# Scaling v on VectorE in place of Pool, with a refitted order model and new ranks, in a fused DeltaNet and low-rank mixer kernel

## The chip, the cores and the metric

The kernel runs on one core of one Trainium2 chip. The metric is the device time of one execution in microseconds. The time before is the median of three runs.

## The reference

Two layers follow each other. The first is a delta-rule attention over 4 batches, 8 heads, 768 steps and a head dimension of 48, the second a mixer over the result, laid out as 4 x 768 x 384:

```
k_n = k / (norm(k) + 1e-6)
for t in range(S):
    y[t]  = q[t] @ state
    v_old = k_n[t] @ state
    state = state + beta[t] * outer(k_n[t], v[t] - v_old)
x = y as (B, S, H*D)
...
h = x^T @ U @ V                       # rank 32, along the sequence
u = x + h^T
out = u + relu(u @ w_ch1) @ w_ch2     # 384 -> 1536 -> 384
```

## The kernel before, in words

The first layer is not run step by step. Chunks of 64 steps are solved at once, and a state is carried from chunk to chunk. The work is cut into 8 units: unit n is one half (six chunks) of batch n // 2, with all its heads. Two large buffers, slot_87 and slot_88 in the profile (both called slot there), hold the even and the odd units.

For a unit, SyncE's queue (SP) loads k, q, v and a second copy of k called z (L367, eight transfers of 72 KB for each of k, q and v, four for z). TensorE (PE) transposes k and q (L463) and makes products of them (L490); k's products give a triangular system. `norms` (L421) takes the norms of k out of the diagonal, makes their reciprocals on VectorE (DVE) and turns the norms into rows (L443); L446 multiplies v in place by those rows, and key "scaled" is then given. In place of dividing k by its norm, the kernel thus scales v. `blocks` (L549) inverts the triangular system: a substitution of pairs of small DVE operations (L581 and L587, 15 pairs in units 0 to 2 and 31 in the others), a transposition (L594), and for units 0 to 2 two further products on PE (L637, L651) whose result DVE takes back (L655, L603). Then PE joins the blocks (L677, L680, L695, L698), ACT copies (L685, L704, L716) and Pool clears corners (L723). `recur` (L732) first prepares each half of a unit (L796 and L807, which need the join, Pool's L723 and the scaled v), and then carries the state: for each chunk PE makes L845 (what the state gives for k), DVE subtracts it from v (z, L858), PE makes L873 from z and DVE adds it to the state (L883; L885 for the first); L760 and L774 make the outputs.

The weights of the second layer arrive as 64-bit floats. `load_weights` (L916) brings 14 slices and DVE rebuilds 32-bit floats in five operations a slice (L974, L980, L986, L992, L1002), with one of ACT (L959). Then, for each of four batches in three blocks of 256 rows, `front` makes the low-rank part (L1025, L1031, L1039, L1043, L1047, L1050), and `wide` the two large products: 36 matmuls of L1117 (72 records, each 32-bit product is recorded twice) and 42 of L1154, the second in a form with seven half-size products that need sums made by DVE (L1089, L1096); L1102 adds the result into X, and L1106 stores it. The PE work of the attention of batches 1 to 3 is placed between the matmuls of the mixer of the batch before.

What is decided ahead of the chip is the order of the instructions on each engine. Each piece of work is a generator that yields an estimated cost before it issues (`op`, L100), or names of results that it needs (`need`). `run` (L198) is a list scheduler with a model of the five engines: it keeps a clock for each, takes the pieces that can start soonest, and among those that start within a small hold (L227) the one with the lowest rank. Ranks come from the call (`place_of`, or a number), or from a table of overrides, PLACES (L140). The model knows [...] PE's change between tile shapes (SWITCH), instruction fetches (LOT, FETCH, `late`), and PE's half clock: `pace` (L176) counts the work in spans of 3.413 us that begin at one assumed phase, PHASE, and multiplies the cost of PE work by 1.9 after a span with little of it. The model never waits on the chip; it only fixes the order, and each engine then runs its queue in that order and waits on semaphores.

Of the kernel before, what the change touches and what calls it, by code (L numbers as in the profile page):

```python
# [26 lines left out]
def kernel(  # L27
# [20 lines left out]
    nc = tc.nc  # L48
# [33 lines left out]


    clock = dict(port=0.0, pe=0.8, dve=0.8, act=0.8, pool=0.8, sp=0.8)
    state = dict(now=0.0, mode=None, hw=0.0, slow=1.9, lot=69, fetched=0.0, flow=0.0, span=0)
    free = dict(pair={x: 0.0 for x in range(4)}, mix={})
    done, parts, waits, ready, last = {}, {}, {}, {}, {}
    asked, missing, awaited, woken = {}, {}, {}, []
    LAT = dict(pe=0.22, dve=0.06, act=0.06, pool=0.1, sp=0.0)
    SWITCH, HOLD = 0.18, 0.18  # L90
    LOT, FETCH = 256, 3.9
    SPAN, PHASE = 3.413, 1.44

    def dve(n):
        return (n + 151) / 960.0
# [17 lines left out]
    def emitted(key, after=0.0):  # L113
        done[key] = state["now"] + after
        for i in awaited.pop(key, ()):
            missing[i].discard(key)
            if not missing[i]:
                woken.append(i)
# [19 lines left out]
            waits[i] = s  # L138

    PLACES = """  # L140
    add_up b0 i0 60.5; add_up b1 i0 12.835; block b0 i1 c2 87.0; block b0 i1 c3 87.0
    block b1 i2 c4 90.229; blocks n1 17.5; diagonals n0 h0 18.353; diagonals n0 h1 18.353
    diagonals n2 h1 89.754; diagonals n3 h1 32.197; gather b0 i1 h1 c1 91.5; gather b1 i0 h0 c1 28.323
    gather b1 i1 h1 c0 28.323; grams n3 i0 -1.0; grams n3 i1 -1.0; grams n4 i0 9.835
    grams n6 i1 30.555; grams n7 i0 8.088; grams n7 i1 17.0; joins n3 h0 43.767
    load n1 namev halves(0, 1) 90.5; load n2 namev halves(0, 1) 90.5; norms n4 95.0; norms n6 17.663
    outputs b0 c0 74.0; outputs b0 c1 86.5; outputs b0 c10 85.5; outputs b1 c2 73.081
    outputs b1 c9 30.481; outputs b3 c0 -9.5; prepare n1 h0 -5.5; prepare n3 h1 58
    prepare n5 h0 -6.5; prepare n5 h1 -6.5; prepare n7 h0 55.06; prepare n7 h1 55.06
    products n1 i1 j1 70.0; products n2 i0 j0 87.293; products n2 i1 j0 39.279; products n2 i1 j1 60.538  # L150
    products n3 i1 j1 12.0; products n4 i1 j0 54.436; recur b1 49.374; recur b2 18.0
    seed n5 10.405; start i2 99.0; wide b0 i0 30.055; wide b2 i1 2.667
    """
    PLACES = dict(x.strip().rsplit(" ", 1) for x in PLACES.replace("\n", ";").split(";") if x.strip())

# [15 lines left out]
        return free[tag], [y for y in free[tag] if x is None or x == y]  # L171

    def cost_of(s):
        return s["cost"] * (state["slow"] if s["mode"] else 1.0)

    def pace(at, end, flow):  # L176

        while int((end - PHASE) / SPAN) > state["span"]:
            state["span"] += 1
            edge = PHASE + SPAN * state["span"]  # L180
            part = flow * min(1.0, max(0.0, (edge - at) / max(end - at, 1e-9)))
            used, flow, at = state["flow"] + part, flow - part, max(at, edge)
            if used > 0.36 * SPAN or "mixing" in done:
                state["slow"] = 1.0
            elif used < 0.28 * SPAN and "mixing" not in done:
                state["slow"] = 1.9
            state["flow"] = 0.0
        state["flow"] += flow

    def late(s, at):  # L190

# [6 lines left out]
    def run():  # L198
        stall = {}
        while waits or woken:  # L200
            while woken:
                i = woken.pop(0)
                at = max([0.0] + [done[x] for x in asked[i]])
                if at > ready[i]:
                    last[i] = None
                advance(i, None, max(at, ready[i]))
            some = {}
            for i, s in waits.items():
                e, was = s["e"], last.get(i)
                at = max(was[1] if was and was[0] == e else ready[i], clock[e])  # L210
                if s["port"]:
                    at = max(at, clock["port"])
                if s["take"]:
                    banks, of = places(s)
                    if not of:
                        continue
                    at = max(at, min(banks[y] for y in of))
                if s["mode"] and s["mode"] != state["mode"]:
                    at += SWITCH
                stall[i] = late(s, at)[1]  # L220
                some.setdefault(e, []).append((at + stall[i], i))
            picks = []
            for e, them in some.items():
                soon = min(at for at, _ in them)
                them.sort(key=lambda x: (not waits[x[1]]["rush"], x[1]))
                for at, i in them:
                    hold = 0.18 if i[0] < 13 else HOLD if i[0] < 90 else SWITCH  # L227
                    if at > soon + hold:
                        continue
                    if not any(a < at and a + waits[x]["cost"] < at + 0.05 for a, x in them):  # L230
                        picks.append((at, i))
                        break
            at, i = min(picks)
            at -= stall[i]
            s, got = waits[i], None
            if s["take"]:
                banks, of = places(s)
                got = min(of, key=lambda y: (banks[y], y))
                del banks[got]
            cost = cost_of(s)  # L240
            if s["e"] == "pe":
                crossed, more = late(s, at)
                state["lot"] += s["words"]
                if state["lot"] > LOT:
                    state["lot"] -= LOT
                    cost += more
                    behind = state["hw"] - crossed - more - 2.4
                    state["fetched"] = crossed + more + FETCH + max(0.0, behind)
                pace(at, at + cost, s["flow"])
            state["now"] = clock[s["e"]] = at + cost  # L250
            if s["port"]:
                clock["port"] = at + cost
            if s["mode"]:
                state["mode"] = s["mode"]
            for tag, x in s["give"]:
                free[tag][x] = state["now"] + s["lat"]
            last[i] = s["e"], state["now"]
            advance(i, got, state["now"] + s["lat"])
# [162 lines left out]
    def norms(n):  # L421

        _, _, _, _, _, vn, _, _ = units[n]
        b, hf = divmod(n, NU)
        flat = gs.rearrange("p s t -> p (s t)")
        yield need(("laid", n), ("seeded", n))
        yield op("act", 0.2)
        norm = small.tile([128, BK], FP32, name="norm")
        nc.scalar.sqrt(norm, flat[:, 0 : BK * BK : BK + 1])
        yield need(("betas", hf))  # L430
        yield op("dve", 1.15, port=True)
        nc.vector.tensor_scalar_add(norm, norm, 1e-6)
        rec = small.tile([128, BK], FP32, name="rec", bufs=1)
        nc.vector.reciprocal(rec, norm)
        nc.vector.tensor_tensor(out=rec, in0=rec, in1=rec, op=ALU.mult)
        nc.vector.tensor_tensor(out=cp[:, n % 2], in0=rec, in1=betas[:, hf, b], op=ALU.mult)
        nc.vector.tensor_copy(
            out=xt.rearrange("p s t -> p (s t)")[:, 0 : BK * BK : BK + 1], in_=cp[:, n % 2]
        )
        emitted(("c", n))  # L440
        yield op("dve", 0.2)
        rows = small.tile([128, BK], FP32, name="norm_rows")
        nc.vector.transpose(rows, norm)  # L443
        yield landed("v", n)
        yield op("pool", 2.2)
        nc.gpsimd.tensor_tensor(  # L446
            out=vn.rearrange("p c (r j) d -> p r c j d", r=2),
            in0=vn.rearrange("p c (r j) d -> p r c j d", r=2),
            in1=rows[:, 0:CS].rearrange("p (r c j) -> p r c j", r=2, c=UC)[
                :, :, :, :, None  # L450
            ].to_broadcast([128, 2, UC, 2, D]),
            op=ALU.mult,
        )
        emitted(("scaled", n), 0.2)

    def grams(n, i):
        kn, kq, pg, qk, qn, _, diag, _ = units[n]
# [91 lines left out]
    def blocks(n):  # L549
# [26 lines left out]
        nc.vector.tensor_tensor(out=gb, in0=gb, in1=by, op=ALU.mult)  # L576
        for j in range(size - 1):
            m, w = j + 1, size - 1 - j
            yield op("dve", 2 * dve(split * m * w), port=True)
            prod = single.tile([128, split, m, w], FP32, name="prod", tag="prod")  # L580
            nc.vector.tensor_tensor(  # L581
                out=prod,
                in0=gb[:, :, j : j + 1, j + 1 :].to_broadcast([128, split, m, w]),
                in1=xb[:, :, 0:m, j : j + 1].to_broadcast([128, split, m, w]),
                op=ALU.mult,
            )
            nc.vector.tensor_tensor(  # L587
                out=xb[:, :, 0:m, j + 1 :], in0=xb[:, :, 0:m, j + 1 :], in1=prod,
                op=ALU.subtract,
            )  # L590
# [625 lines left out]
```

## Time and profile before

| | us |
|---|---|
| median of 3 runs | 626.62 (626.53 to 628.6) |
| the profiled execution | 629.01 |
| its span, first to last instruction | 627.2 |
| PE busy | 589.1 (94%) |
| DVE busy | 393.7 (63%) |
| ACT busy | 227.4 (36%) |
| POOL busy | 47.3 (8%) |
| first matmul of the mixer's first product (L1117) | starts at 114.93 |
| mean granted clock of TensorE | 0.940 |

The profile tells one execution. Busy times are sums over an engine's instructions; a share is of the span, and says nothing on which stage an engine bounds. A line such as L446 is a line of the kernel; out<-in are tile names, 128x1152 is partitions by elements, and a number in brackets at a line's end is how long the engine was idle ahead of it and what ended that. 64*64 ahead of a matmul's shape is the part of the array that it uses. The changed file is 13 lines longer from the order model on, so that its L459 stands for L446 of this one.

### The profile page before, as it was taken

Reading aid. Unit: us, or ns where it says so; the run is one execution under the profiler, and the core shown is the slowest. Engines: PE = TensorE matmul, PEld = TensorE weight load, DVE = VectorE, ACT = ScalarE, POOL = GpSimd, SP = SyncE. Lnnn points to the kernel's source line nnn. Section 1 sums busy time; section 2 is a strip of 40 time slices with the busy share of each in tenths; the row PEclk is TensorE's granted clock in tenths of the full one; section 3 lists DMA queues with packets and bytes.
Section 4 is the critical chain, followed back from the end, with each engine's and each line's share of the span. In section 5 each row is a group of like instructions: output and inputs, shape, how many; then the busy total and the mean of one; then the engine's idle time right before and its main releaser. Section 6 shows DMA issues by size and latency. Waiting matters only on the chain.

```text
span 627.2 us, 23410 instructions
## 1 busy us (share of the span) xinstructions
PE 589.1 (94%) x10536; PEld 519.3 (83%) x10536; DVE 393.7 (63%) x957; ACT 227.4 (36%) x450; POOL 47.3 (8%) x69
## 2 busy tenths in 40 slices
PE   5598879899989999999999999999999999999997
PEld 5498867688779888888887878898989869898987
DVE  4979877988989528998995883459923123131312
ACT  3745556522252553255147227331130431101020
POOL 3031010001200100013002001010000000000000
PEclk9855557999989999999999999999999999999999
DMA  8570666750000050450043034000000000000000
GB/s 125 104 160 4 204 172 145 183 125 28 3 4 5 28 97 3 93 102 8 15 82 68 3 74 80 12 24 6 1 26 14 17 2 2 25 1 27 13 13 26
DMA packets 101572, 33.26 MB, mean 53 GB/s; under 512 B 90528, under 2 KB 101280, under 8 KB 101472
## 3 DMA queue, kind: packets, MB, share of 16 engines
q1 hardware_dynamic: 99712, 31.18, 22.1%
q8 instruction: 82, 1.34, 0.8%
q10 hardware_dynamic: 1600, 0.30, 0.3%
q0 software_dynamic: 160, 0.30, 0.2%
q14 instruction: 18, 0.15, 0.1%
HBM read 27.03 MB, written 4.72 MB: 51 GB/s over the span
## 4 chain that ended last, share of the span: by engine, by line
PE 72%; DVE 20%; issue 3%; ACT 2%; DMA 1%; SPq 1%; DVEq 0%; ACTq 0%
PE P L1154 24%; PE P L1117 23%; DVE xt L587 5%; DVE prod L581 5%; PE P L490 3%; PE P L796 2%; PE P L463 2%; PE P L845 2%; PE P L1039 2%; PE P L807 2%; PE P L873 2%; PE P L637 2%; DVE zz L594 2%; PE P L651 2%; PE P L760 1%
## 5 line engine op out<-in xcount | busy, mean ns | idle before, releaser
L1117 PE MATMUL P<-ut,w_sb 128*128 128x256 f32 x864 | 202.1, 387 | 0.6 <-ACT ut L1050 0.6
L1117 PEld LDWEIGHTS P<-ut,w_sb 128*128 128x128 f32 x864 | 161.4, 192 | 24.4 <-issue 1.2
L1154 PE MATMUL P<-w_sb,hs 128*128 128x192 f32 x720 | 125.9, 329 | 0.4 <-DVE X L1102 0.4
L1154 PEld LDWEIGHTS P<-w_sb,hs 128*128 128x128 f32 x720 | 117.2, 190 | 3.5 <-DVE X L1102 0.7
L1073 ACT ACTIVATE hs<-P 128x512 f32<-128x512 f32 x72 | 43.0, 597 | 149.7 <-PE P L1117 138.2
L587 DVE TENSOR_TENSOR xt<-xt,prod 128x112 f32<-128x112 f32 (+21 forms) x200 | 64.6, 323 | 6.9
L581 DVE TENSOR_TENSOR prod<-gs,xt 128x112 f32<-128x112 f32 (+21 forms) x200 | 64.4, 322 | 4.8
L1102 DVE TENSOR_TENSOR X<-X,P 128x192 f32<-128x192 f32 x84 | 29.5, 351 | 60.0 <-PE P L1154 59.3
L1089 DVE TENSOR_TENSOR S<-hs 128x384 f32<-128x384 f32 x24 | 16.7, 694 | 63.3 <-ACT hs L1073 63.3
L744 ACT COPY X<-P 64x192 f32<-64x192 f32 x96 | 30.0, 313 | 71.6 <-PE P L774 67.3
L1154 PE MATMUL P<-w_sb,S 128*128 128x192 f32 x288 | 51.1, 330 | 0.0
L1154 PEld LDWEIGHTS P<-w_sb,S 128*128 128x128 f32 x288 | 46.7, 190 | 1.1
L463 PE MATMUL P<-ident,slot 128*128 128x128 f32 x192 | 29.4, 304 | 10.9 <-POOL xt L566 5.1
L858 DVE TENSOR_TENSOR z<-slot,P 128x192 f32<-128x192 f32 x44 | 15.5, 353 | 37.7 <-PE P L845 27.8
L716 ACT COPY slot<-zz 32x384 f32<-32x384 f32 x64 | 32.6, 509 | 10.9 <-DVE zz L594 6.9
L463 PEld LDWEIGHTS P<-ident,slot 128*128 128x128 f32 x192 | 24.3, 156 | 14.2 <-POOL xt L566 5.1
L490 PEld LDWEIGHTS P<-slot 48*64 48x64 f32 x1536 | 27.2, 145 | 5.2 <-ACT slot L478 2.4
L490 PE MATMUL P<-slot 48*64 48x64 f32 x1536 | 30.3, 232 | 0.9 <-ACT slot L478 0.7
L446 POOL TENSOR_TENSOR slot<-slot,norm_rows 128x1152 f32<-128x1152 f32 x8 | 19.9, 2482 | 145.2 <-DVE norm_rows L443 57.4
L1050 ACT COPY ut<-P 128x384 f32<-128x384 f32 x24 | 10.6, 479 | 42.8 <-PE P L1047 33.3
L478 ACT COPY slot<-P 128x768 f32<-128x768 f32 x30 | 23.0, 805 | 8.3 <-PE P L463 8.1
L883 DVE TENSOR_TENSOR s<-s,P 128x192 f32<-128x192 f32 x40 | 14.0, 351 | 13.6 <-PE P L873 12.0
(116 smaller groups left out, 735.9 us busy)
## 6 DMA issues: line engine op xcount, KB each, us to landing
slot<-in_k_dram SPq DMA_DIRECT2D x92, 72.0 KB, 2.9
slot<-in_q_dram SPq DMA_DIRECT2D x64, 72.0 KB, 3.0
slot<-in_v_dram SPq DMA_DIRECT2D x64, 72.0 KB, 2.7
out_dram<-X SPq DMA_DIRECT2D x24, 192.0 KB, 1.9
X<-in_moe_w_ch_dram SPq DMA_DIRECT2D x10, 384.0 KB, 4.2
wide<-in_moe_w_ch_dram SPq DMA_DIRECT2D x10, 384.0 KB, 3.5
hs<-in_moe_w_ch_dram SPq DMA_DIRECT2D x4, 384.0 KB, 4.9
wide<-in_moe_V_dram SPq DMA_DIRECT2D x4, 192.0 KB, 3.9
```

What stands on the lines that cost most here:

```text
L446: nc.gpsimd.tensor_tensor(out=vn.rearrange("p c (r j) d -> p r c j d", r=2), in0=vn.rearrange("p c (r j) d -> p r c j d", r=2), in1=rows[: ...
L463: nc.tensor.transpose(p_t[:, c // 3, c % 3], t[:, c, 2 * j : 2 * j + 2].rearrange("p s d -> p (s d)"), ident,)
L478: nc.scalar.copy(to, p_t)
L490: nc.tensor.matmul(p_g[half(g ^ (par * i)), par, c], kq[rows, c, j, 0, half(g)], kq[rows, c, j, i, half(g)], start=True, stop=True,)
L581: nc.vector.tensor_tensor(out=prod, in0=gb[:, :, j : j + 1, j + 1 :].to_broadcast([128, split, m, w]), in1=xb[:, :, 0:m, j : j + 1].to_bro ...
L587: nc.vector.tensor_tensor(out=xb[:, :, 0:m, j + 1 :], in0=xb[:, :, 0:m, j + 1 :], in1=prod, op=ALU.subtract,)
L716: nc.scalar.copy(pg[quarter(i), :, at, :, a : a + BK], cut(zc, h)[quarter(i)].rearrange("p r (c j) t -> p r c j t", j=2),)
L744: nc.scalar.copy(x[half(c % 2), c // 2, 4 * D * g : 4 * D * (g + 1)].rearrange("p (j r d) -> p r j d", r=2, d=D), states(p_y)[half(g)],)
L1073: nc.scalar.activation(hs[:, fs[0] : fs[1] + 1 : fs[1] - fs[0]], p_f, ACTF.Relu)
L1102: nc.vector.tensor_tensor(out=to, in0=to, in1=p, op=ALU.add)
L1117: nc.tensor.matmul(p_f[:, fs.index(f)], w1_sb[:, y, 256 * t + 128 * fs.index(f) :][:, 0:128], ut[:, t], start=(t == 0), stop=(t == KT - 1),)
L1154: nc.tensor.matmul(p_o, a[:, f], w2_sb[:, w, f], start=(first and f == 0), stop=(f == HF - 1), skip_group_check=True,)
```

## The change

It has three parts. The multiplication of v by the norms (L446) goes from Pool to DVE, with a cost for the model of 1.37 on DVE's clock in place of 2.2 on Pool's. The model keeps three copies of the clock's account, for three phases of the spans, and uses their mean slowness; it also accounts idle PE time, fetch constants and the cost of a substitution pair differently, and lets ranks under 13 reach further ahead. And the table of ranks is replaced as a whole, 48 entries before and 83 after. No other operation is added or taken away, and tiles, buffers and transfers are the same.

```diff
-    SPAN, PHASE = 3.413, 1.44
+    SPAN, PHASES = 3.413, (0.3, 1.4, 2.5)
...
-    LOT, FETCH = 256, 3.9
+    LOT, FETCH = 256, 4.1
...
-    add_up b0 i0 60.5; add_up b1 i0 12.835; block b0 i1 c2 87.0; block b0 i1 c3 87.0
+    add_up b2 i0 20.634; block b0 i1 c2 22.0; block b0 i1 c3 21.5; block b1 i1 c2 35.866
...
-        return s["cost"] * (state["slow"] if s["mode"] else 1.0)
+        return s["cost"] * (sum(state["slow"]) / 3 if s["mode"] else 1.0)
...
-        while int((end - PHASE) / SPAN) > state["span"]:
+        for y, phase in enumerate(PHASES):
+            since, rest = at, flow
+            while int((end - phase) / SPAN) > state["span"][y]:
...
-                    hold = 0.18 if i[0] < 13 else HOLD if i[0] < 90 else SWITCH
+                    hold = 0.9 if i[0] < 13 else HOLD if i[0] < 90 else SWITCH
...
+            if s["e"] == "pe":
+                pace(at, at, 0.0)
...
-                    behind = state["hw"] - crossed - more - 2.4
-                    state["fetched"] = crossed + more + FETCH + max(0.0, behind)
+                    behind = max(0.0, state["hw"] - crossed - more - 0.5)
+                    state["fetched"] = crossed + more + FETCH + 0.6 * behind
...
-        yield op("pool", 2.2)
-        nc.gpsimd.tensor_tensor(
+        yield op("dve", 1.37, port=True)
+        nc.vector.tensor_tensor(
             out=vn.rearrange("p c (r j) d -> p r c j d", r=2),
...
-        emitted(("scaled", n), 0.2)
+        emitted(("scaled", n), 0.1)
...
-            yield op("dve", 2 * dve(split * m * w), port=True)
+            yield op("dve", 2 * dve(split * m * w) + 0.04, port=True)
```

More of the change, by code (lines that the diff above doesn't have):

```diff
@@ L84 @@
     clock = dict(port=0.0, pe=0.8, dve=0.8, act=0.8, pool=0.8, sp=0.8)
-    state = dict(now=0.0, mode=None, hw=0.0, slow=1.9, lot=69, fetched=0.0, flow=0.0, span=0)
+    state = dict(now=0.0, mode=None, hw=0.0, slow=[1.9] * 3, lot=69, fetched=0.0, flow=[0.0] * 3, span=[0] * 3)
     free = dict(pair={x: 0.0 for x in range(4)}, mix={})
@@ L140 @@
     PLACES = """
-    add_up b0 i0 60.5; add_up b1 i0 12.835; block b0 i1 c2 87.0; block b0 i1 c3 87.0
[L142 to L152, printed above, removed]
+    add_up b2 i0 20.634; block b0 i1 c2 22.0; block b0 i1 c3 21.5; block b1 i1 c2 35.866
@@ new lines @@
+    block b1 i1 c3 35.866; block b1 i2 c4 35.866; block b1 i2 c5 35.866; block b2 i0 c0 20.5
+    block b2 i0 c1 13.818; block b2 i1 c2 20.5; block b2 i1 c3 20.5; block b2 i2 c4 20.5
+    block b2 i2 c5 20.5; block b3 i0 c0 47; block b3 i0 c1 47; block b3 i1 c2 61.5
+    block b3 i1 c3 45; block b3 i2 c4 74.223; block b3 i2 c5 32.219; blocks n0 1.5
+    blocks n4 31.5; blocks n5 39.961; diagonals n0 h1 62.521; diagonals n2 h1 76.126
+    diagonals n4 h1 24.134; gather b0 i0 h0 c0 26.825; gather b0 i0 h1 c0 26.825; gather b0 i0 h1 c1 26.825
@@ new lines @@
+    gather b0 i1 h0 c0 26.825; gather b0 i1 h1 c0 26.825; gather b0 i1 h1 c1 26.825; gather b1 i1 h0 c1 68.79
+    gather b2 i0 h0 c0 94.933; gather b2 i0 h0 c1 94.933; gather b2 i0 h1 c0 94.933; gather b2 i0 h1 c1 94.933
+    grams n4 i1 88.043; grams n5 i0 16.17; joins n0 h0 7.09; joins n4 h0 7.5
+    joins n6 h0 15.795; last_sum b0 i1 49.575; last_sum b2 i0 57.639; load n0 nameq halves(0, 1) 18
+    load n0 namez halves(0, 1) 62.0; load n1 namez halves(0, 1) 6.5; load n2 namek halves(0, 1) 91.212; load n2 namev halves(0, 1) 37.366
@@ new lines @@
+    load n3 nameq halves(0, 1) 78; load n4 nameq halves(0, 1) 56.473; load n5 namez halves(0, 1) 4.5; load n7 nameq halves(0, 1) 0.5
+    load_beta u1 70.633; load_weights 78.54; norms n3 7.0; norms n4 98.768
+    norms n5 99.142; outputs b0 c0 20.134; outputs b0 c2 20.134; outputs b0 c3 73.223
+    outputs b0 c4 76.156; outputs b0 c5 101.407; outputs b0 c7 20.134; outputs b1 c0 18.0
+    outputs b1 c10 85.126; outputs b1 c9 -5; outputs b2 c1 72.723; outputs b3 c0 62.5
+    outputs b3 c1 62.5; outputs b3 c6 64.5; prepare n2 h0 -3.5; prepare n2 h1 -3.5
@@ L153 @@
+    products n1 i0 j1 73.29; products n2 i1 j0 67.0; products n2 i1 j1 67.0; products n4 i1 j1 1.5
+    products n6 i1 j0 -4.31; products n7 i1 j0 68.29; products n7 i1 j1 63.79; recur b0 6.5
+    relu b0 i0 87.433; start i1 68; wide b2 i1 82.5
     """
@@ L173, in cost_of @@
     def cost_of(s):
-        return s["cost"] * (state["slow"] if s["mode"] else 1.0)
+        return s["cost"] * (sum(state["slow"]) / 3 if s["mode"] else 1.0)
     def pace(at, end, flow):
-        while int((end - PHASE) / SPAN) > state["span"]:
[L179 to L188, printed above, removed]
+        for y, phase in enumerate(PHASES):
+            since, rest = at, flow
+            while int((end - phase) / SPAN) > state["span"][y]:
+                state["span"][y] += 1
+                edge = phase + SPAN * state["span"][y]
+                part = rest * min(1.0, max(0.0, (edge - since) / max(end - since, 1e-9)))
+                used, rest, since = state["flow"][y] + part, rest - part, max(since, edge)
+                if used > 0.36 * SPAN or "mixing" in done:
+                    state["slow"][y] = 1.0
+                elif used < 0.28 * SPAN:
+                    state["slow"][y] = 1.9
+                state["flow"][y] = 0.0
+            state["flow"][y] += rest
     def late(s, at):
```

## The prediction

> **What bounds the kernel now.** I read the page first (TensorE, PE, is busy 589.1 us of 627.2), then the busy time by stretches, cut where the record of PE's granted clock changes.
>
> ```profile
> 26.60:77.80 51.20, 42.56 (x1232) 40.35 (x1233) 43.82 (x101) 26.49 (x55) 8.61 (x10) 0.50 0.48 122
> 77.80:81.20 3.40, 2.46 (x100) 2.14 (x98) 3.25 (x6) 1.56 (x3) 0.00 (x0) 1.00 0.74 232
> 81.20:101.70 20.50, 15.70 (x480) 14.46 (x484) 15.19 (x28) 10.76 (x22) 2.05 (x4) 0.50 0.59 143
> ...
> 176.80:180.20 3.40, 3.40 (x24) 2.71 (x15) 3.06 (x11) 1.78 (x4) 0.01 (x1) 0.50 0.03 7
> 180.20:623.70 443.50, 439.35 (x7158) 387.04 (x7156) 243.54 (x615) 142.83 (x290) 24.60 (x34) 1.00 0.14 30
> ```
>
> Columns: stretch, length, busy time of PE, weight loads, VectorE (DVE), ACT, POOL, then the granted clock. From 180 us to 623.7 PE idles 4 us in 443: there the time is the sum of PE's work. Before 108.9 (first L1025, the mixer's start) PE is at half clock for some 72 us and waits on chains through DVE. So there are four places to look: the front stage, the amount of PE work behind it, changes of array tile inside that work, and the few PE waits.
>
> The longest PE wait behind the front lies at 174 us. The timeline there:
>
> ```profile
> 168.54 1.18 DVE L576 TENSOR_TENSOR gs<-gs,cp 128x1024 f32<-128x1024 f32 x1
> 168.83 2.87 POOL L446 TENSOR_TENSOR slot<-slot,norm_rows 128x1152 f32<-128x1152 f32 x1 [3.83 <-DVE norm_rows L443]
> 169.64 2.48 DVE L1089 TENSOR_TENSOR S<-hs 128x384 f32<-128x384 f32 x1
> ...
> 174.02 0.53 DVE L655 SCALAR_TENSOR_TENSOR zz<-P,upper_rows,zz 128x96 f32<-128x96 f32 x2
> 174.38 0.24 PE L677 MATMUL P<-zz,slot 32*32 32x32 f32 x2 [1.40 <-DVE zz L655]
> ```
>
> and the same L1089 over the whole run:
>
> ```profile
> L1089 DVE TENSOR_TENSOR S<-hs x24: 519/558/2475, 138.4 to 610.8; 128x384 f32<-128x384 f32 x24
> L446 POOL TENSOR_TENSOR slot<-slot,norm_rows x8: 2120/2450/2952, 32.3 to 419.5; 128x1152 f32<-128x1152 f32 x8
> ```
>
> L1089 takes 0.56 us, but 2.48 beside POOL's L446. That 1.92 us makes L655 late, PE waits 1.40 and then 0.59 more, and the next stretch (176.8 to 180.2) is at half clock: 12 matmuls of L1117 take 4.41 us to the next group, where 12 x 0.216 = 2.59 is usual. Together 3.8 us.
>
> Two more views: POOL's queue at the first scaling of unit 1, with PE behind it, and the price of a tile change.
>
> ```profile
> 45.13 2.12 POOL L446 TENSOR_TENSOR slot<-slot,norm_rows 128x1152 f32<-128x1152 f32 x1 [9.76 <-ACT slot L704]
> 47.31 0.88 POOL L723 MEMSET slot<- 32x384 f32 x2
> 47.77 1.50 PE L796 MATMUL P<-slot 64*64 64x64 f32 x30 [0.76 <-POOL slot L723]
> ```
>
> ```profile
> 353.54 2.22 PE L1154 MATMUL P<-w_sb,S 128*128 128x192 f32 x12
> 355.69 0.45 PE L845 MATMUL P<-s,slot 48*64 48x48 f32 x16
> 355.95 0.41 PE L774 MATMUL P<-z,slot 64*64 64x48 f32 x16
> 356.19 0.41 PE L760 MATMUL P<-s,slot 48*64 48x48 f32 x16
> 356.68 0.40 PE L873 MATMUL P<-z,slot 64*48 64x48 f32 x16
> 357.01 2.22 PE L1154 MATMUL P<-w_sb,hs 128*128 128x192 f32 x12
> ...
> 474.96 4.07 PE L1154 MATMUL P<-w_sb,S 128*128 128x192 f32 x24
> ```
>
> Unbroken, 24 matmuls of L1154 go from 474.96 to 478.86, 0.1625 each, so 12 need 1.95; ahead of a recurrence step they hold PE 2.15 (353.54 to 355.69). The last small group needs 0.33 to the next L1154 against 0.23 inside, the first 0.27. An excursion from the full array and back costs 0.20 + 0.10 + 0.04 = 0.34, so 0.17 a change. L760 to L873 is 0.49 instead of 0.23: L873 waits 0.26 for the z that DVE makes from L845 of the same excursion.
>
> [...] 2.48 against 0.56 above, while L1102 and L521, which read PSUM, keep their 0.35 and 0.55 beside L446. [...] Here POOL takes 2.12 to 2.95 for 1152; no scaling on DVE is in this trace. [...] The clock's changes here at 77.8, 81.2, 176.8 and 180.2 are 3.4 or whole multiples apart. [...]
>
> **The change, part by part.** Costs are differences against the profiled execution, 629.01 us (span 627.2); the median shown is 626.62, 2.4 lower, and I apply the difference to that.
>
> *Scaling on DVE.* Eight L446 leave POOL (19.9 us) and come to DVE. Price: L576 of 1024 elements takes 1.18, and 128 elements more at its rate of about 1 ns make 1.31 each[...]. That is 10.5 us on an engine busy 63%. Ends: at best it costs nothing and frees DVE's own stalls (1.9 at 169, 1.5 at 290, 0.3 at 46); at worst all of it lies in front of something PE waits for. Six of the eight lie behind 130 us, beside PE work. There I summed DVE's work and PE's work in the new order from L1031 and L1025 on. L594 of unit 2 ends at 50.1 of DVE's sum against 52.4 of PE's at L637 (before: 48.5 against 49.7); its L655 at 57.5 against 62.1 at the L677 behind (before 56.6 against 58.9). The margins grow[...]. I take the wait at 174 and its slow window as gone: -3.8 (0 to -4). Late next is again L594 of unit 2, by a margin of about 2.
>
> *First two scalings.* These lie on DVE's early chain. In the new order of the SP queue unit 0's v loads are issues 41 to 48. Before, 40 issues took 29.1 us, 0.73 each, so the last is issued by 35.9 and lands 2.4 later (as before, 29.9 to 32.3): 38.2. DVE arrives there at about 36.4 and waits 1.8; queued behind are L655 and L603 of unit 0 and the whole substitution of unit 1. But L655 ran at 39.1 before, so only 0.4 passes on; with the second scaling and beta's transpose, part of which hide behind PE's L651, L594 of unit 1 ends about 0.7 later than 58.2. On the other side L723 no longer stands behind L446: L796 of unit 0 may start near 45.6 instead of 47.8, and the first two recurrence steps run ahead.
>
> *Front stage in sum.* Between that L594 and L1031 DVE has 43.9 us of work before and took 52.8 (8.9 idle). The new order holds 45.6: two L521 more, one small weight slice, two L974 and one L980 more, one L883 and four L503 less. With no idle L1031 stands at 104.5, with 8.9 idle at 113.4; before it was at 111.0. As most of the idle pieces there are waits on recurrence groups, now partly ahead, I take 6: 110.5, so -0.5 (-6.5 to +2.4).
>
> *Order of PE.* Behind the first L1025 the new order has six more transposes L463 (6 x 0.109 = 0.65) and 48 more matmuls L490 (96 records of 0.016 = 1.54), deferred from the front: +2.2. Changes of tile shape behind that point go from 160 to 176: 16 x 0.17 = +2.7 (bounds 0.10 to 0.25 a change: 1.6 to 4.0). Steps in which L873 follows its own L845 in one excursion without other filling go from 13 to 9: -4 x 0.26 = -1.0. The transposes of unit 3's q, which waited 0.8 for their load at 125 us, now stand behind more of L1117: -0.8.
>
> *The model's other numbers* (three window phases, instruction fetch, 0.04 more on a substitution pair) give no instruction; they act only through the order just counted.
>
> *Waits of the new order that I cannot see.* PE's other waits behind 128 us sum to some 4 us now. I allow 1 more (0 to 5).
>
> Sum: -3.8 - 0.5 + 2.2 + 2.7 - 1.0 - 0.8 + 1.0 = -0.2. So 628.8 for such a profiled execution, 626.4 for the median.
>
> **The rivals.**
> *Slower: the clock stays low to the mixer's start.* Before, the clock rose for good at 101.7, behind a window (98.3 to 101.7) with twelve L463 in a row; L845, L774 and L760 then needed 0.27 in place of 0.43. The new order has those transposes in three lots of six, the first two recurrence steps from the end. If neither they nor the L796 and L807 of unit 1, now closer together, fill a window, three steps of five small groups cost 0.17 more each (2.5), and L1025, L490 and L1039 behind them run at half speed (1.4 + 0.8 + 1.3): +5 to +6, about 632. It decides from the point where the clock is still 0.5 when L1025 starts. For it: of the 21 windows at half clock before 101.7 only two were followed by full clock. Against: one of those two held just L796 and L807.
> *Faster: the recurrence runs ahead.* If DVE's idle time in the front falls to about 1, L1031 stands near 105.5: 5 more, about 621.5. For it: steps 1 and 2 no longer wait 13 us between their L845 (54.6 to 67.7). Against: unit 1's joins are not earlier, and the last three steps need them.
> [...] If another wait takes the place of that at 174, 3.8 come back: 630.
> *v lands late.* Each us beyond 38.2 delays everything behind DVE's first scaling: 2 us late gives 628.4.
>
> **How the numbers follow.** Half a percent, 3.1 us, is about what a measurement here can tell from no change: 623.5 to 629.7. The likeliest case, 0.42, is no change, and its sum gives 626.4. Faster 0.25 (its centre 621.5), slower 0.33 (the clock 0.25[...]). To leave out two in ten the range reaches into both: 620.5 to 633.5.
>
> **What would show it.** Right: no POOL L446; eight DVE multiplications of 1.3 us; L1089 never above 0.6; no PE wait for L655 over 0.5 and no half clock after 130 us; L1031 at 109 to 112; the excursions' 0.34 unchanged. Wrong: a DVE scaling that waits over 3 us, half clock at L1025, or new PE waits behind 130 us that sum to more than 9 us.

## The result, and the profile after

The changed kernel takes 633.49 us (median of 4 runs, 632.17 to 634.49; the profiled execution 634.49, its span 632.8) where the kernel before took 626.87 beside it (626.53 to 628.6). The ratio is 1.0097, interval 1.0073 to 1.0121: 6.1 us slower by the ratio (the two medians lie 6.6 apart). The forecast was no change, 626.4. Lines of the kernel after that lie behind the order model are 13 higher than before: L446 is L459, L463 is L476, L1025 is L1038, L1117 is L1130.

Busy time by stretches of the kernel after, columns as before (stretch, length, PE, weight loads, DVE, ACT, POOL, granted clock, share of the DMA engines, GB/s):

```profile
108.43:115.25 6.82, 6.08 (x67) 3.53 (x68) 3.48 (x6) 2.04 (x3) 0.00 (x0) 0.50 0.80 191
115.25:135.74 20.49, 17.54 (x176) 13.59 (x175) 18.16 (x30) 10.10 (x17) 0.00 (x0) 1.00 0.92 200
135.74:139.15 3.41, 3.36 (x13) 2.71 (x12) 1.53 (x3) 2.22 (x3) 0.00 (x0) 0.50 0.12 25
139.15:629.30 490.15, 484.94 (x7921) 425.20 (x7919) 290.67 (x719) 155.49 (x313) 16.07 (x33) 1.00 0.13 29
```

The half clock at 176.8 is gone, but there are two new ones: over the mixer's start, and at 135.7. The PE timeline at both places:

```profile
109.17 1.51 PE L476 MATMUL P<-ident,slot 128*128 128x128 f32 x6 [1.82 <-DMA slot<-in_k_dram]
110.61 2.78 PE L1038 MATMUL P<-X,u_sb 128*32 128x384 f32 x12
...
135.16 2.11 PE L476 MATMUL P<-ident,slot 128*128 128x128 f32 x10 [2.29 <-DMA slot<-in_q_dram]
```

Each of the two half clocks stands beside a wait of the transposes L476 for a load: 1.82 for unit 2's k, 2.29 for unit 3's q. Before, PE took up unit 2's k without a wait, and waited 0.78 for that q:

```profile
98.39 2.82 PE L463 MATMUL P<-ident,slot 128*128 128x128 f32 x12
...
125.06 0.87 PE L463 MATMUL P<-ident,slot 128*128 128x128 f32 x6 [0.78 <-DMA slot<-in_q_dram]
```

A second wait of 0.81 follows there at 126.75, for which the profile names no load. In the chain of work that ended last (section 4 of the page) SP's queue has 7% of the span after, 1% before.

What was moved, and what the scaling itself does (columns: shortest, median and longest duration in ns, first and last start):

```profile
L1102 DVE TENSOR_TENSOR S<-hs x24: 548/558/559, 133.1 to 616.4; 128x384 f32<-128x384 f32 x24
```

```profile
L459 DVE TENSOR_TENSOR slot<-slot,norm_rows x8: 1357/1358/1359, 38.0 to 444.0; 128x1152 f32<-128x1152 f32 x8
```

The eight scalings take 1.36 each (1.31 was forecast), and L1102, the L1089 of before, never exceeds 0.56.

Taken apart at the mixer's first group: it starts at 110.61 instead of 108.94 (+1.7), and from there to PE's last end it takes 518.70 instead of 514.74 (+4.0).

**The queue of loads.** SP's timeline shows its loads in the order in which they were written. In the kernel before:

```profile
92.90 6.23 SPq L367 DMA_DIRECT2D slot<-in_q_dram  x8
99.18 3.18 SPq L367 DMA_DIRECT2D slot<-in_k_dram  x4
...
118.10 6.37 SPq L367 DMA_DIRECT2D slot<-in_q_dram  x8
124.57 1.22 SPq L952 DMA_DIRECT2D wide<-in_moe_w_ch_dram  x2
```

and after:

```profile
99.87 7.36 SPq L380 DMA_DIRECT2D slot<-in_k_dram  x10
...
121.72 1.96 SPq L380 DMA_DIRECT2D slot<-in_k_dram  x3
...
126.04 1.57 SPq L965 DMA_DIRECT2D wide<-in_moe_w_ch_dram  x2
127.72 5.30 SPq L380 DMA_DIRECT2D slot<-in_q_dram  x8
133.06 1.29 SPq L380 DMA_DIRECT2D slot<-in_k_dram  x2
```

A load named z also reads in_k: it is the copy of k with its halves exchanged, four DMAs for a unit, and only the recurrence reads it, in after first at 194.3 us. Before, unit 2's z are the four at 99.18, behind its k and q, and unit 3's z come behind the last weight slice (124.57), its q ahead of that. After, the ten at 99.87 are unit 2's four z and then six of its k; the last two of its k are issued at 133.06. Unit 3's z (one in a group left out here, three at 121.72) are ahead of its q, and so are three loads of v (123.73, left out) and the last weight slice at 126.04. So loads that nobody waits for stand ahead of loads that PE waits for. Two entries of the new table place them so: unit 2's k has rank 91.212 and unit 3's q has 78, while the z of these units keep the ranks of the call, 31 and 35, and the lower rank goes first. The order model's own clock, worked out by running it, has unit 3's last q issued at 127.6 and PE's first transposes of it done at 131.0; SP was done with the q at 133.0. The model counts 0.65 for each issue on SP, and the trace has 0.66 for these eight (5.30 in all), so the lag of 5.4 built up ahead of them; where is not worked out.

**Theories.** *Late loads*: the rank order delays k and q on SP, and with them PE and its clock. *Clock*: the new order of the recurrence leaves the array at half clock at the mixer's start (the slower rival of the prediction), and the load is a bystander. *PE's work*: changes of tile and deferred groups are the loss. *Scaling*: VectorE's own 1.36 a unit costs the front.

### The profile page after: what moved, and what is told of

Its sections match the earlier page's. It is cut to its first block, busy times and chain, and to the rows that moved or that the text cites. A ratio compares the mean times of both kernels' runs of the same rounds, so it can differ in the third digit from the quotient of the medians.

```text
span 632.8 us, 23372 instructions
## 1 busy us (share of the span) xinstructions
PE 595.7 (94%) x10536; PEld 521.6 (82%) x10536; DVE 401.7 (63%) x965; ACT 228.2 (36%) x450; POOL 27.0 (4%) x61
## 4 chain that ended last, share of the span: by engine, by line
PE 75%; DVE 10%; SPq 7%; DMA 4%; issue 3%; ACT 1%; ACTq 0%; DVEq 0%
PE P L1130 26%; PE P L1167 26%; SPq L380 7%; PE P L858 2%; PE P L503 2%; DMA slot<-in_k_dram 2%; PE P L476 2%; PE P L809 2%; PE P L886 2%; PE P L773 2%; PE P L1052 2%; PE P L820 2%; PE P L664 2%; DVE xt L600 2%; DVE prod L594 2%
## 5 line engine op out<-in xcount | busy, mean ns | idle before, releaser
L1130 PE MATMUL P<-ut,w_sb 128*128 128x256 f32 x864 | 202.8, 386 | 0.0
L1130 PEld LDWEIGHTS P<-ut,w_sb 128*128 128x128 f32 x864 | 160.0, 191 | 22.3
L1102 DVE TENSOR_TENSOR S<-hs 128x384 f32<-128x384 f32 x24 | 13.4, 556 | 68.1 <-ACT hs L1086 68.1
L476 PE MATMUL P<-ident,slot 128*128 128x128 f32 x192 | 33.3, 328 | 14.3 <-POOL xt L579 5.2
L476 PEld LDWEIGHTS P<-ident,slot 128*128 128x128 f32 x192 | 26.8, 169 | 19.7 <-issue 9.0
L503 PEld LDWEIGHTS P<-slot 48*64 48x64 f32 x1536 | 29.3, 153 | 8.0 <-ACT slot L491 4.5
L503 PE MATMUL P<-slot 48*64 48x64 f32 x1536 | 33.0, 241 | 2.9 <-ACT slot L491 2.4
L858 PEld LDWEIGHTS P<-s,slot 48*64 48x64 f32 x704 | 16.2, 148 | 9.4 <-issue 6.2
```

The lines of the kernel that those rows point to most:

```text
L476: nc.tensor.transpose(p_t[:, c // 3, c % 3], t[:, c, 2 * j : 2 * j + 2].rearrange("p s d -> p (s d)"), ident,)
L503: nc.tensor.matmul(p_g[half(g ^ (par * i)), par, c], kq[rows, c, j, 0, half(g)], kq[rows, c, j, i, half(g)], start=True, stop=True,)
L858: nc.tensor.matmul(states(p_b)[half(g ^ par), par, j], kq[half(par, D), cu, j, 0, half(g)], states(s_old)[half(par, D), g, j], start=True, ...
L1130: nc.tensor.matmul(p_f[:, fs.index(f)], w1_sb[:, y, 256 * t + 128 * fs.index(f) :][:, 0:128], ut[:, t], start=(t == 0), stop=(t == KT - 1),)
```

## Experiments

Differences below are ratios to the kernel before, run on the same chip in the same set.

**Scaling alone, in both orders** (b_dve, a_pool, b_mix, a_mix). The call is given to the other engine at its written place, so that nothing else moves:

```diff
-        nc.gpsimd.tensor_tensor(
+        nc.vector.tensor_tensor(
             out=vn.rearrange("p c (r j) d -> p r c j d", r=2),
```

for b_dve (the order of before), the reverse for a_pool (the order of after), and `(nc.vector if n >= NU else nc.gpsimd)` for b_mix and a_mix.

b_dve: 

> The order of before, with only the eight scalings issued by VectorE at the places where the order model had them on Pool. [...] both stalls and the half clock after the first go: 626.9 - 3.8 = about 623, less if the first scaling (v landed at 32.3) delays the front by its 1.36 each. Rival (another wait takes the place at 174): 626 to 628. The second scaling stands ahead of unit 1's substitution here and may cost up to 1.4 of the front.

a_pool: 

> The order of after, with only the eight scalings put back on Pool. If moving them to VectorE is worth 3 to 4 us by itself in this order too, about 637. If the scaling is worth nothing in this order: 633.5. If VectorE's own time in the front is what made after slow [...]: below 632.

b_mix: 

> The order of before, with the scalings of units 2 to 7 on VectorE and those of units 0 and 1 on Pool. The runs with all eight on VectorE had 2.3 less behind the mixer's start and a mixer that started 2.5 later. If the first two scalings in VectorE's chain delay the front, this keeps the gain alone: 2 to 4 below before, 623 to 626. If the later start was a matter of the clock's windows in that one execution, it equals the run with all eight: 0 to 0.5 below before.

a_mix: 

> The order of after, with the scalings of units 0 and 1 on Pool and those of units 2 to 7 on VectorE. If the first two cost the front: 1 to 2.5 below after and at or below the run with all on Pool (1.0056 of before). If they cost nothing: equal to after (1.0097).

Measured: b_dve 0.9994 (0.9981 to 1.0008), b_mix 0.9991 (0.9967 to 1.0015), a_pool 1.0056 (1.0033 to 1.0078), a_mix 1.0066 (1.0033 to 1.0098). By itself the scaling is worth nothing that can be measured in the order of before: -0.4 us, between -1.2 and +0.5. I had expected that putting it back makes after slower; it doesn't, and whether a_pool is really 2 us below after can't be told, since the intervals overlap. In the mixed kernels, with the first two scalings on Pool and the other six on VectorE, nothing is gained either, so the front does not pay a clear price for the first two. Why the stall at 174 us was not worth 3.8 is seen in the timeline of b_dve:

```profile
173.26 0.55 DVE L1089 TENSOR_TENSOR hs<-hs 128x384 f32<-128x384 f32 x1
174.19 1.35 DVE L446 TENSOR_TENSOR slot<-slot,norm_rows 128x1152 f32<-128x1152 f32 x1
175.93 0.53 DVE L655 SCALAR_TENSOR_TENSOR zz<-P,upper_rows,zz 128x96 f32<-128x96 f32 x2
176.29 0.24 PE L677 MATMUL P<-zz,slot 32*32 32x32 f32 x2 [0.75 <-DVE zz L655]
```

In before the first operation of L1089 took 2.48 at 169.64 and 2.01 at 291.60, each beside an L446 of Pool; those are the two stalls. Here, with no L446 on Pool, all three of L1089 at this place are at 0.55 to 0.56 (172.20 to 173.26). What it is in Pool's operation that holds L1089 is not shown; L576 at 290.04 in before keeps its 1.18 with an L446 beside it from 290.25 on. But the scaling itself now stands ahead of L655 in VectorE's queue: of the 1.92 saved 1.35 is given back, and PE still waits 0.75 (1.40 before) and then the same 0.59. That leaves a gain of 0.65, which the measured -0.4 can hold, and no half clock at this place. This profile has a half clock at the mixer's start (111.7 to 118.6) with no wait for a load beside it, and the profile of b_mix has none from 97.0 on, so the order of before can meet a half clock there too.

**The kernel before once more** (b_again, no edit).

> A second profiled execution of the kernel before. If the half clock at 176.8 to 180.2 belongs to the wait at 174, it is there again with the 4.41 us of L1117. If it depends on where the clock's windows of 3.4 us happen to lie to that wait, it may be gone, while the wait of 1.4 and 0.6 stays.

Its waits at the place are the same, 1.40 and 0.59, L1089 takes 2.48 beside L446 again, and yet there is no half clock in this execution; a stretch of its clock record:

```profile
100.80:623.00 522.20, 509.00 (x8326) 445.25 (x8320) 313.04 (x762) 172.67 (x343) 31.14 (x39) 1.00 0.17 39
```

Twelve L1117 behind the wait are through in 2.86 (4.41 to the next group in the first profile), and from the mixer's start to PE's end it takes 512.56 in place of 514.74. So the half of the 3.8 that was clock comes in some executions only. Of four profiles with this pair of waits three have it (before; b_zfirst and e_tile below, at 181.9 and 179.3), and b_again has not. In the records of before and after the stretches between changes of the clock are whole multiples of 3.413 us (51.20 in before is 15 of them), and the 522.20 above is 153. Counted in such steps from a change, before has 1.57 us of the two waits in one step, with half clock behind it; b_again has 1.26 and 0.74 on both sides of an edge, and no half clock. b_again is a single profiled execution, 625.76.

**u_sb earlier** (a_usb). Three VectorE instructions of the first weight slice, which the new order puts behind unit 1's substitution, are issued behind unit 0's square root instead; their costs in the model stay where they were, so that all else keeps its order.

```diff
         nc.scalar.sqrt(norm, flat[:, 0 : BK * BK : BK + 1])
+        if n == 0:
+            early[0](0, powers0[0])
...
-            nc.vector.scalar_tensor_tensor(
+            if i:
+                nc.vector.scalar_tensor_tensor(
```

> The order of after, with only three VectorE instructions of the first weight slice (L999, L1005, L1015 of u_sb) issued at about 17.5 us instead of 59.9, so that the room they free lets the queue of loads go on at 41 instead of 60. Theory late data: the weights and the loads of units 2 and 3 behind them on SP come earlier, the waits of L476 for k (1.8) and q (2.3, and about 0.9 of half clock behind it) and VectorE's 4.3 of waits for weights shrink: about 629. Theory order of PE (tile changes, deferred work) or clock set by the recurrence: 633 to 634, no change.

Measured 1.0087 (1.0058 to 1.0116), no change against after. SP's timeline says why:

```profile
40.23 0.93 SPq L969 DMA_DIRECT2D X<-in_moe_w_ch_dram  x2
...
98.19 8.56 SPq L380 DMA_DIRECT2D slot<-in_k_dram  x10
...
127.69 5.30 SPq L380 DMA_DIRECT2D slot<-in_q_dram  x8
```

One weight slice comes 20 us earlier, the next is not issued before 64.5, the z and k are 1.7 us earlier, and q is where it was. My first theory of the late loads, that u_sb had delayed the whole queue, fell here.

**k and q from another queue** (a_kq).

```diff
-                queue.dma_start(
+                (nc.gpsimd if (name, n) in (('k', 2), ('q', 3)) else queue).dma_start(
```

> The order of after, with only the eight loads of unit 2's k and the eight of unit 3's q issued from Pool's queue instead of SP's, at the same places of the written order. Theory late data through SP's queue: the waits of L476 at 109 (1.8) and 135 (2.3 and 0.9 of half clock) go, the half clock at the mixer's start may go with the first: 628 to 630. Theory slots freed late (the loads wait for the memory, not for the queue): the waits stay, 633. Theory order of PE: 633.

Measured 1.012 (1.01 to 1.0139): slower still. The waits moved. SP's timeline of a_kq, and PE's:

```profile
110.35 10.21 SPq L380 DMA_DIRECT2D slot<-in_k_dram  x9
```

```profile
122.11 2.79 PE L476 MATMUL P<-ident,slot 128*128 128x128 f32 x12 [3.18 <-DMA slot<-in_k_dram]
```

The q that Pool issued from 106.4 on was in time, the clock was full at the mixer's start (107.1) and the wait at 135 was gone. But beside it SP's nine loads from 110.35 (unit 3's k and one z) took 10.2 in place of 6.0, and PE waited 3.18 for them. Another new wait, of 1.91 for VectorE's L1044, ends at 111.38; behind each of the two comes a half clock (111.5 to 114.9 and 121.7 to 125.1). From 98 to 109 us and from 109 to 122 a_kq moved 149 and 174 GB/s and after 103 and 201: over both together about as much, 162 and 156, only earlier. The edit moves the loads to another engine's queue as well, and no run parts this from the order. So the run shows that k and q can be in time at the mixer's start and that another load is then late; it doesn't price the queue.

**z behind the loads that PE waits for** (a_again, a_z, a_z2, a_zA, a_zB). The DMAs of z are kept back and sent later; the order of every engine but SP stays word for word that of after. The edit of a_z2:

```diff
-                queue.dma_start(
+                (put.append if name == "z" and n in (2, 3) else send)(dict(
...
+        list(map(send, put if (name, n) == ("k", 2) else ()))
```

a_z has `("q", 3)` in the last line; a_zA keeps back unit 2's z alone, a_zB unit 3's alone. a_again is the kernel after without an edit, as their base.

a_again: 

> The kernel after, unchanged, as the base for the others on this chip. 1.0097 of the time before (about +6), with the waits of L476 for its loads (1 to 2.3 us at 109 and at 135) in any execution if they belong to the order; without them in some if the clock's windows decide.

a_z: 

> The order of after, with only the eight loads of the second copies of k (z) of units 2 and 3 issued behind unit 3's q instead of ahead of unit 2's k, of unit 3's k and q. Nothing else moves; z is read only 100 us later. Theory late data (the rank order puts loads nobody waits for ahead of those PE waits for): unit 2's k lands 2.6 earlier, unit 3's q 5.2 earlier; the waits at 109 (1.8), 135 (2.3) and the half clock behind it (0.9 to 1.7) go: 4 to 5 below after, about 629. Theory order of PE (tile changes and deferred groups, a front that ends later): no change against after.

Measured: a_again 1.009 (1.0057 to 1.0122), a_z 1.0116 (1.0084 to 1.0148). The profile of a_again repeats both waits, 2.17 for unit 2's k and 1.52 for unit 3's q, and the half clock over the mixer's start (109.0 to 115.9), but has no half clock behind the wait for q. In a_z there is no gain, but its profile had no wait for q and a mixer that started at 106.2. PE's timeline of a_z, and SP's:

```profile
134.43 0.85 PE L476 MATMUL P<-ident,slot 128*128 128x128 f32 x6 [4.47 <-DMA slot<-in_k_dram]
```

```profile
119.51 6.13 SPq L352 DMA_DIRECT2D slot<-in_q_dram  x8
125.69 6.64 SPq L352 DMA_DIRECT2D slot<-in_k_dram  x10
```

I had sent the eight z ahead of the last two loads of unit 2's k (the ten at 125.69), and PE waited 4.47 for those. The same error as the rank order's, made by hand.

a_z2: 

> As the kernel a_z, but the eight loads of z are now issued behind the last two loads of unit 2's k too: in a_z these two stood behind the eight and PE waited 4.47 for them at 134 us, with a half clock behind it, while its other waits for loads were gone and the mixer began at 106.2. Theory late data: that wait goes too, 4 to 6 below a_z, which is 3 to 5 below after: about 629 on the chip of the first result. Theory that PE's work in the new order (4.3 more behind the mixer's start) is the whole loss: as after.

Measured 0.9982 (0.9968 to 0.9997): 6.8 us below a_again (0.0108 of 627; by the two intervals some 4.5 to 9), and a little below the kernel before. PE's timeline of a_z2 at the places of the lost time:

```profile
118.95 1.64 PE L476 MATMUL P<-ident,slot 128*128 128x128 f32 x12 [0.72 <-DMA slot<-in_k_dram]
131.42 0.85 PE L476 MATMUL P<-ident,slot 128*128 128x128 f32 x6 [0.52 <-DVE S L1102]
```

and its clock:

```profile
106.00:628.20 522.20, 508.91 (x8239) 443.57 (x8237) 317.13 (x763) 172.46 (x340) 16.04 (x33) 1.00 0.17 39
```

At both places no wait for a load over 0.72; the mixer starts at 108.91, and no half clock from 106.0 on, with PE's order unchanged. So the half clock at the mixer's start does not come with PE's order alone.

a_zA: 

> The order of after with only unit 2's z (four loads) issued behind unit 2's last k; unit 3's z stays ahead of unit 3's q. All loads from unit 2's k on are issued 2.6 us earlier. If the mixer's start is what counts: most of the gain of a_z2 (0.998 to 1.001 of before). If the two moves count alike: half, 1.003 to 1.004. If unit 3's q is what counts and needs both: 1.004 to 1.007.

a_zB: 

> The order of after with only unit 3's z (four loads) issued behind unit 2's last k. Unit 3's q is issued 2.6 us earlier, unit 2's k is not: the wait before the mixer's start (1.8 to 2.2) stays, the wait for q at 135 (1.5 to 2.3) and a half clock behind it go. Half of the gain: 1.003 to 1.005 of before. If only the mixer's start counts: 1.008.

Measured: a_zA 1.0024 (1.0008 to 1.004), a_zB 1.0042 (1.0027 to 1.0056). Against a_again that is 4.1 and 3.0 us, each with some 2.3 either way, 7.1 together, where both moved at once gave 6.8. The remaining wait of a_zA, then of a_zB:

```profile
130.10 1.83 PE L476 MATMUL P<-ident,slot 128*128 128x128 f32 x12 [1.48 <-DMA slot<-in_q_dram]
```

```profile
109.22 1.51 PE L476 MATMUL P<-ident,slot 128*128 128x128 f32 x6 [1.89 <-DMA slot<-in_k_dram]
```

a_zA has the mixer start at 106.6 at full clock and waits once more, 1.38 for unit 3's k at 117; a_zB starts at 110.7, with a half clock, and has no wait for q.

**The same misplacement in the order of before** (b_zfirst), and its cure there (b_zd).

```diff
                 yield op(e, 0.65, port=False)
+                if (name, n, g, s) in (("k", 2, 0, 0), ("q", 3, 0, 0)):
+                    for gg in halves:
+                        for ss in (1, 3):
+                            nc.sync.dma_start(
+                                out=units[n][7][half(1 - gg), :, ss // 2, 0:D],
...
+                if name == "z" and n in (2, 3):
+                    emitted((name, n, g, s // 2), landing(384))
+                    continue
```

b_zfirst: 

> The kernel before with the four loads of unit 2's z issued ahead of unit 2's k and those of unit 3's z ahead of unit 3's q, as after has them; nothing else moves. If late loads are what made after slow, the same misplacement costs here too: unit 2's k and q and unit 3's q land 2.6 later, of which some is slack: 1.003 to 1.008 of before. If the order of before has slack for it: 1.000.

Measured 1.0095 (1.0064 to 1.0126): eight DMAs moved, nothing else, and the kernel before is as slow as the kernel after. PE's timeline of b_zfirst (L475 is the transpose):

```profile
100.93 1.52 PE L475 MATMUL P<-ident,slot 128*128 128x128 f32 x6 [3.19 <-DMA slot<-in_k_dram]
...
130.71 2.79 PE L475 MATMUL P<-ident,slot 128*128 128x128 f32 x12 [3.62 <-DMA slot<-in_q_dram]
```

It shows waits for the same two loads, here ahead of the last recurrence steps and at 130, and a half clock behind the second (130.7 to 134.1; another at 181.9, behind the wait that before has at 174). The mixer starts at 111.8.

b_zd, the order of before with unit 2's z behind unit 3's loads and all scalings on VectorE: 

> The order of before with all scalings on VectorE and with the four loads of unit 2's z issued behind the loads of unit 3 in place of ahead of them. If what PE waits for at 125 to 128 us (0.8 and 0.8 for q) and VectorE's waits for weights ahead of it come from SP's queue, 1.5 to 3 below before: 624 to 625.5. If these waits move elsewhere: equal to before.

Measured 0.9979 (0.9961 to 0.9996): 1.3 us. The waits for q at 125 fell to 0.55 and 0.32. It doesn't part the z from the scaling, which alone had 0.9994.

**Both cures** (a_best: a_z2 with the edit of a_usb).

> The kernel a_z2 (z behind the loads that PE waits for) with u_sb's three instructions at 17.5 us instead of 59.9. If their place in VectorE's queue (1.1 us ahead of unit 1's joins) counts once the loads are in time: 0.996 to 0.997 of before. If not: as a_z2, 0.998.

Measured 1.0 (0.9979 to 1.0021); the interval of a_z2 overlaps this one. No gain of u_sb's place is seen here either.

**The price of a change of tile** (e_tile). In the kernel before, in the middle of each L1154 group:

```diff
+                if f == HF // 2:
+                    nc.tensor.matmul(
+                        P[0:64, 0, 384:432], ident[0:64, 0:64], ident[0:64, 0:48],
+                        start=True, stop=True, skip_group_check=True,
+                    )
```

> The kernel before with one extra small matmul (64 x 64 weights, 48 columns, into columns that nobody reads) in the middle of each of the 84 groups of L1154: 84 more excursions from the full array and back, 168 changes of tile. At the 0.34 an excursion that the prediction read from the trace: 84 x 0.34 = 28.6, and about 0.02 a matmul: 655 to 657. If a change of tile costs nothing and only the matmul counts: 628 to 630.

The extra matmul changes sums of the result; only its time is read. Measured 1.0707 (1.0682 to 1.0732): 44.4 us for 84 excursions, 0.53 each, above the 0.34 of the prediction. One of them in the timeline:

```profile
559.79 1.47 PE L1154 MATMUL P<-w_sb,S 128*128 128x192 f32 x8
561.18 0.31 PE L1159 MATMUL P<-ident 64*64 64x48 f32 x2
561.43 0.92 PE L1154 MATMUL P<-w_sb,S 128*128 128x192 f32 x4
```

From start to start, a mean over the excursions: 0.256 to the small one, 0.093 between its two records, 0.148 back, 0.267 for the first L1154 behind it: 0.76, where two L1154 unbroken take 0.325. That is 0.44, with the small matmul's own time in it. 84 of them make 37 us; of the other 7 some 5 are more of PE's waits in this kernel (13.4 against 8.3 behind the mixer's start, gaps over 0.25), and there is one more half clock (517.2 to 520.6). The prediction had the same pieces, but counted its 0.20 over a whole group and less for the small part.

## Why the prediction was wrong, step by step

*Scaling on VectorE, -3.8.* Its prices were right (1.36 against 1.31; unit 0's v landed at 38.0 against 38.2; VectorE waited 1.7 against 1.8), the stall of L1089 went (2.48 before, at most 0.56 after), and after has no wait at that place. The size failed: alone the move gives -0.4. Half of the 3.8 was a half clock that follows the same waits in some executions and not in others (b_again has none), and the other half needs an order in which the scaling does not itself stand ahead of L655 (b_dve).

*Front stage, -0.5 (-6.5 to +2.4).* It summed VectorE's work and left the loads of unit 2's k out. In the profile of after, VectorE's first L1044 (L1031 in before) stands at 113.6, where 110.5 was forecast. VectorE's work ahead of it was foreseen (44.8 us against 45.6); its idle time was not, 10.9 against 6. In the profiles of after's order with unit 2's z out of the way (a_z, a_z2, a_zA, a_best) that idle time is 5.4 to 7.6, so the 6 was right for loads in time; where the z stay ahead of k in SP's queue (after, a_again, a_zB, a_pool, a_mix, a_usb) it is 9.5 to 10.9. PE's wait for k set the mixer's start.

*Order of PE, +2.2 + 2.7 - 1.0 = +3.9.* The sum was right. Two profiles that are at full clock from the mixer's start on tell it: from there to PE's end, less the waits over 0.25, b_again has 512.56 - 7.59 = 504.97, a_z2 514.31 - 5.78 = 508.53: +3.6. Two more on each side (b_mix 504.4 and b_zd 504.9; a_best 509.0 and a_zA 509.1) make it +4.1 in the mean. How the sum splits is not tested. The price of a change was somewhat low: 0.22 in the trace of e_tile, inside the bounds of 0.10 to 0.25, and 0.26 by its device time.

*"The transposes of unit 3's q, which waited 0.8 for their load at 125 us, now stand behind more of L1117: -0.8."* **This is the step that failed with its sign.** I moved the transposes and not their load: the eight DMAs of q had been moved behind unit 3's z, three loads of v and the last weight slice, from 118.1 to 127.7. The transposes waited 2.29, and a half clock followed.

*"Waits of the new order that I cannot see": +1.0 (0 to 5).* **This is the step that failed by its size**, and here unit 2's k belongs, for which the prediction had no term. These waits could be seen, in the order of SP's queue, of which I had counted only unit 0's v. Unit 2's k and unit 3's q measured 4.1 and 3.0 apart, 6.8 together (a_zA, a_zB, a_z2), in place of -0.8 + 1.0 = +0.2, and the reverse edit costs before 6.0 (b_zfirst).

*The slower rival* came near the right time (632) by luck, for another reason. Its sign was there, half clock as L1038 starts at 110.61, and its lots of six transposes too; but a_z, a_zA and a_z2, with the same order of PE, start the mixer at full clock. Three profiles with a wait for k of 1.82 to 2.17 there (after, a_again, a_zB) start it at half clock, and in a_mix, with 1.84, the clock falls 0.6 us behind the start. (The window ahead of 77.8, which this rival says held just L796 and L807, ends with L873 and L651 as well.)

*The balance.* The loads cost 6.8 and the whole change 6.1, so with its loads in time the new order should come out near the time of before, and a_z2 does (-1.1). PE's work is longer by 4.1, so something gives it back. The profiles point to two places. The waits over 0.25 behind the mixer's start sum to 5.5 in a_z2 and a_best, against 8.0 in before and b_again: 2.5. And the mixer starts earlier: at 107.2 in the mean of a_z, a_z2, a_zA and a_best (106.2 to 108.9), against 109.5 in six profiles of the order of before (107.4 to 111.4; before, b_again, b_dve, b_mix, b_zd, e_tile): 2.3. This is an estimate from single profiles that scatter by some 2 us, and no run tests it by itself.

## What to carry to other kernels

When a planner writes the order anew, read each DMA queue that issues its loads as written, as SP's does here, like an engine: for every load its issue, what stands ahead of it, and when the first reader comes. A load that is read last must not stand ahead of one that is waited for, and a model whose queue runs ahead of the real one (127.6 against 133.0 here) does not show the wait that this brings. Take from a single profile no clock effect that a second profile of the same kernel doesn't show.

## What the runs showed of the hardware

- In before the waits of 1.40 and 0.59 were followed by 3.4 us of half clock (176.8 to 180.2), in b_again, the same kernel, by none. From the mixer's start to PE's end the two profiles take 514.74 and 512.56.
- In the trace of before, cut from the mixer's start on into steps of 3.413 us counted from a change of its clock record, PE's gaps over 0.25 us sum to 1.57 in one step at full clock and to at most 1.02 in any other. Half clock followed the one with 1.57 and none of the others. In after one such step has 2.29 (132.3 to 135.7), with half clock behind it, and no other over 1.09; none of those was followed by half clock.
- In a_kq Pool's queue issued ten loads from 106.4 to 113.1 us. SP's nine loads from 110.35 on took 1.13 us each to issue there; in after the ten from 99.87 took 0.74 each and the eight from 127.72 took 0.66.
- In e_tile the first full-array matmul (L1154) behind a small one takes longer to the next one as well: 0.267 from start to start, in place of 0.1625, beside the 0.256 of the one ahead.
